# GpSimd takes the elementwise preparation of early chunks, and chunk 5's keys come as rows

## The chip, the cores and the metric

The kernel runs on one core of a Trainium2 chip. The core has five engines with a queue each, worked off in order: TensorE (PE in the profile: matrix products; PEld is its loading of weights), VectorE (DVE), ScalarE (ACT), GpSimd (POOL) and SyncE (SP, which issues DMAs here). The metric is the device time of one execution in microseconds. Three executions of the kernel before took 847.1, 846.52 and 846.56 us, median 846.56.

## The reference

Three parts, one feeding the next, all in float32. First a linear attention with decay over 4 batches, 8 heads, 768 steps and 48 channels:

```
for t in range(S):
    cur = einsum(u * k[t], v[t])
    y[t] = einsum(r[t], state + cur)
    state = w * state + einsum(k[t], v[t])
```

Its output, 3072 tokens of 384 numbers, goes through a maximum of three products (`max(x@w1, x@w2, x@w3) @ w_out`, 768 wide) and then through a mixture of 8 experts in which each token goes to the two best of its noisy gates.

## The kernel before, in words

**Chunks and blocks.** The tokens are cut into 24 chunks of 128 (six to a batch). Attention works by chunk. The middle part works by block of three chunks (8 blocks). Block b runs 21 units: 18 steps `u_step` (a product for each of six column groups f and three weights j; k = 3f + j) and three steps `x2_step`, units 18 to 20, that multiply by `w_out` and the gates. While block b runs, the attention of later chunks is put between its units by a table BURSTS: at unit (b, k) stand the output of one chunk and the scores of the next. For block 0 these are (0,2): output 3, scores 4; (0,9): output 4, scores 5; (0,17): output 5, scores 6.

**Preparing a chunk.** `prep1(g)` makes two tiles on VectorE: `Pk`, k times a table of decays (L389), and `Rp`, r times another (L390). `prep2(g)` makes what the state and the bonus (the term with u) need. For chunks below NPE = 6 it makes r times k (L401, tile `t1`), and then `keys(g)` lets TensorE turn and scale the keys with a diagonal matrix (L430, 16 products) and sum the bonus (L435, 16 products); ScalarE copies the result (L436) and scales v by it (L443). For later chunks the keys come from memory as rows in a tile `ldt` (L247) and VectorE does all: product of r and k (L406), the keys times a table (L408), times u (L409), the sum by head (L410), times v (L411, tile `sv`). The table is made in units 9 and 12 of block 0. The output of a chunk is taken out of PSUM with `sv` added (L498). The last chunk of a batch, as chunk 5, passes on no state.

**Weights.** In block 0 VectorE also decodes the 24 weight tiles (L1568 to L1570, three instructions each, generator `conv`) and subtracts the high parts that ScalarE makes (L672) to get the low parts (L673, generator `splits`). A counter `room` decides how many such instructions `fill` emits in a unit. Block 0's `u_step` multiplies in full float32 (L734); its results are taken out by ScalarE for j = 0 (L741) and by a maximum on VectorE for j = 1 and 2 (L745, tile `uw`); after j = 2 ScalarE makes `hHt` (L747) and VectorE `hLt` (L749), which the `x2_step` reads (L765 to L767; it needs the last group in its last three products). Later blocks use L736 to L738.

**Order.** Everything is in the order in which the program emits it (a manual schedule): each engine's queue holds its instructions in that order. In blocks 0 and 1 a generator `agen` of preparation instructions is advanced once a unit, or as often as STEPS says for that unit, and is emptied every seven units; loads of chunk g + 2 are issued at those units too, through SP's queue, in which a load waits until its buffer is free and holds up what is behind it. POOL makes constants at the start and issues the scatters of rows to the experts, six per block.

Of the kernel before, what the change touches and what calls it, by code (L numbers as in the profile page):

```python
# [34 lines left out]
CAPS = (816, 848, 816, 800, 784, 784, 768, 768)  # L35
ROW = DM + E + 1
NWST = 12
NPE = 6


BURSTS = {(0, 2): ([3], [4]), (0, 9): ([4], [5]), (0, 17): ([5], [6]), (1, 2): ([6], [7]), (1, 9): ([7], [8]),
# [3 lines left out]
PLAIN = (8,)  # L45
XTR = 19
TURN = 5
STEPS = {(0, 1): 2, (0, 2): 0, (1, 8): 2, (1, 10): 0}
SCATTER = 11
FLAGS = 5  # L50
TABK = 12
# [23 lines left out]
def gap(k):  # L75

    k = k.rearrange("p (a c) -> p a c", a=4)
    return bass.AP(tensor=k.tensor, offset=k.offset, ap=[k.ap[0], [DP, 4], [64, 2], [1, 48]])
# [125 lines left out]
def moe_kernel(ctx, tc, rT, kT, tm, wuT, wrow, urow, mw, wout, wgn, noise, ew1, ew2, out):  # L204
    nc = tc.nc
    v = nc.vector
# [22 lines left out]
    def cols():  # L229

        return at.tile([128, DM], F32, name="cols", bufs=6)

    def load_rk(g, eng=nc.sync):

        l = LD[g] = Ctx()
        l.r = at.tile([DP, 4, 128], F32, name="ldr", tag="ldr", bufs=3)
        (nc.sync if g < 2 else eng).dma_start(l.r, rT[:, g])
        l.k = at.tile([DP, 4, 128], F32, name="ldk", tag="ldk", bufs=3)
        eng.dma_start(l.k, kT[:, g])

    def load_tv(g, eng=nc.sync):

        l = LD[g]
        rows = tm[g * C:(g + 1) * C]
        if g >= NPE:
            l.t = at.tile([128, DM + 4 * DP], F32, name="ldt", tag="ldt", bufs=2)
            eng.dma_start(l.t, rows[:, :DM + 4 * DP])  # L247
        l.v = cols()
        eng.dma_start(l.v, rows[:, DM + 4 * DP:])

    def load(g, eng=nc.sync):
        load_rk(g, eng)
        load_tv(g, eng)
# [90 lines left out]
    Tr, Tk = T[:, :, 0:128], T[:, :, 127::-1]  # L344
# [35 lines left out]
    def hd(ap):  # L380
        return ap.rearrange("p (h d) -> p h d", h=H)

    def prep1(g):

        l = LD[g]
        a = A_[g] = Ctx()
        a.Pk = at.tile([DP, 4, 128], F32, name="Pk", bufs=2)
        a.Rp = at.tile([128, 4, 128], F32, name="Rp", tag=f"Rp{int(g > 9 and g // 2 % 2)}", bufs=2)[:DP]
        yield v.tensor_mul(a.Pk, l.k, Tk)  # L389
        yield v.tensor_mul(a.Rp, l.r, Tr)  # L390

    def prep2(g):

        l, a = LD[g], A_[g]
        a.v = l.v
        a.K2 = at.tile([128, 4 * DP + 8], F32, name="K2", bufs=2)
        a.sv = at.tile([128, DM], F32, name="sv", bufs=2)
        t1 = at.tile([128, 512], F32, name="t1", tag="t1")
        if g < NPE:
            a.t1 = t1[:DP].rearrange("p (a c) -> p a c", a=4)  # L400
            yield v.tensor_mul(a.t1, l.r, l.k)  # L401
            return
        t1 = t1[:, :DM]
        tr, tk = l.t[:, :DM], l.t[:, DM:DM + 4 * DP]
        red = at.tile([128, H, 1], F32, name="red")
        yield v.tensor_mul(t1.rearrange("p (a b d) -> p a b d", a=4, b=2),  # L406
                           tr.rearrange("p (a b d) -> p a b d", a=4, b=2), gap(tk))
        yield v.tensor_mul(a.K2[:, :4 * DP], tk, TAB["k"])  # L408
        yield v.tensor_mul(t1, t1, ub)  # L409
        yield v.tensor_reduce(red, hd(t1), axis=AX.X, op=OP.add)  # L410
        yield v.tensor_mul(hd(a.sv), hd(a.v), red.to_broadcast([128, H, D]))  # L411

    def prep(g):

        yield from prep1(g)
        yield from prep2(g)
        if g < NPE:
            keys(g)
            if g > 3:
                yield  # L420
            yield
            bonus(g)
# [15 lines left out]
    def bonus(g):  # L438

        a = A_[g]  # L440
        for h in range(H):
            hs = slice(h * D, h * D + D)
            nc.scalar.activation(a.sv[:, hs], a.v[:, hs], AF.Copy, scale=a.K2[:, 4 * DP + h:4 * DP + h + 1])  # L443
# [218 lines left out]
    split_done = [0]  # L662
# [13 lines left out]
    splits = split_all()  # L676

    def until(gen, done, n):
        while done[0] < n and next(gen, gen) is not gen:
            pass  # L680
# [580 lines left out]
    order = list(FEED)  # L1261
    agen, ahead = iter(()), None

    def splits_may(k):

        return 24 if k > 16 else min(len(WGT) + 2, 6) if WGT else 0
# [15 lines left out]
    for b in range(NBLK):  # L1282
        side = {}

        def add(k, fn):
            side.setdefault(k, []).append(fn)

        for k, i in XSK.get(b, {}).items():
            add(k, lambda i=i: init_xs(i))
        if b in (2, 3):  # L1290
            for i in range(OUTP // 2):
                add(4 * i + 1, lambda i=i + (b - 2) * (OUTP // 2): init_out(i))
        for g, q in TURNS.items():
            if q // 21 == b:
                add(q % 21, lambda g=g: x_turn(g))
        if b == NBLK - 1:
            ats.close()
            pools[0] = fast.enter_context(tc.tile_pool(name="ma", bufs=1, side="right"))
            e_alloc(0)
            for i in range(3):  # L1300
                add(2 * i, lambda i=i: e_load(0, i))
            for i in range(8):
                add(3 + 2 * i, lambda i=i: e_high(0, i))
                add(4 + 2 * i, lambda i=i: e_low(0, i))
                if i + 3 < 8:
                    add(4 + 2 * i, lambda i=i: e_load(0, i + 3))
            add(8, lambda: g_load(0, 0))
            add(17, lambda: g_gate(0, 0))
            for k in range(3):
                add(16 + k, lambda k=k: g_tr(0, 0, k))  # L1310
                add(17 + k, lambda k=k: g_low(0, 0, k))
        for k, (kind, f, j) in enumerate(units):
            ready = []
            unit[0] = k
            g = 3 * (b + 1) + k // 7
            if b < 2 and k % 7 == 0:
                load(g + 2)
                drain(agen)
                agen = ahead or prep(g + 1)
                ahead = None  # L1320
            here = BURSTS.get((b, k))
            if here:
                if b > 1:
                    drain(FEED[order.pop(0)].gen)
                if len(here[1]) > 1 or len(here[0]) > 1:
                    while reading[0]:
                        next(rgen)
                    settle()
                ready, late = burst(*here)
                defer.extend(late)  # L1330
            elif b < NBLK - 1 and k == XTR and not bounced(3 * b + 5):
                ready.append(xtr(3 * b + 5))
            if kind and j == 0:
                drain(rgen)
            evs = u_step(b, f, j) if kind == 0 else x2_step(b, j)
            settle()
            if defer and not here:
                defer.pop(0)()
            for fn in side.get(k, []):
                fn()  # L1340
            room = min(max(room, -1.0), 0.5) + ((1.46 if b else 2.3) - 0.47 if kind == 0 else 2.9 if b else 2.2)
            if 1 < b < NBLK - 1:
                room += (2.5 if len(here[0]) > 1 else 1.7) if here else spare(b, k) - ((1.46 - 0.47) if kind == 0 else 2.9)
            elif b < 2:
                room += (1.7 if len(here[0]) < 2 else 2.5) if here else 0.0
                room -= 0.4
            elif k % 2 == 0 and 3 < k < 20:
                room -= 0.9
            if b == 0 and k == 17:

                room = min(room, 0.5)
            if here:
                fill(b, k)
            for fn in ready:
                fn()
            waiting += evs
            if b < 2:
                take(agen, STEPS.get((b, k), 1))
                if k >= XTR and b == 0:
                    ahead = ahead or prep(g + 2)  # L1360
                    next(ahead, None)
            if b and order:
                room -= FEED[order[0]].step(b, k)
            if b == 0:
                until(conv, conv_done, min(k + 2, 18) if k < 13 else min(2 * k - 6, 24))
                if k in (TABK - 3, TABK):
                    tables2()
                for f in GATEM.get(k, ()):
                    wg_mm(f)
                for f in GATEK.get(k, ()):  # L1370
                    wg_tr(f)
                if k == 16:
                    until(splits, split_done, 6)
                    wg_out()
                if k == 17:
                    settle()
                if k == 20:
                    until(splits, split_done, 7)
            if b == 1:
                until(splits, split_done, min(k + 8, 24))  # L1380
            fill(b, k)
        settle()
        settle()
        rgen = route(b)
# [374 lines left out]
```

## Time and profile before

| | |
|---|---|
| median of three runs | 846.56 us |
| the profiled execution | 845.93 us, its span (first to last instruction) 844.1 us |
| TensorE busy | 828.3 us, 98% of the span |
| VectorE busy | 527.3 us, 62% |
| ScalarE busy | 283.7 us, 34% |
| GpSimd busy | 137.5 us, 16% |
| mean granted TensorE clock | 0.997 |

Shares are means over the whole program. Block 0 runs from about 24 to 90 us, block 1 from there to about 140 us. A row of the timeline gives the start, the time from the first start to the last end of the merged instructions, the engine, the line, the operation, what it writes and reads, and in brackets the idle time of that engine just before, with what ended it. VectorE's instructions overlap a little at their ends, so the distance between two starts is the time that one takes of the queue.

### The profile page before, as it was taken

The numbers are of one execution on the slowest core, as the hardware profiler recorded it, in microseconds if no ns is written. First come the engines' busy times: TensorE is split into PE (matmuls) and PEld (weight loads), VectorE is DVE, ScalarE is ACT, GpSimd is POOL, SyncE is SP. The second block draws the span as 40 slices with busy tenths as digits, with TensorE's granted clock in tenths as the row PEclk, the third lists the DMA queues.
The fourth block names the chain that finished last, engine by engine and source line by source line (L and its number), as shares of the span: only waits on it lengthen the run. The fifth ranks groups of instructions, "written<-read, shape, count | busy, mean of one in ns | idle before, by whom it ended". The sixth has DMA issues, their size and how long they took to land.

```text
span 844.1 us, 17138 instructions
## 1 busy us (share of the span) xinstructions
PE 828.3 (98%) x6657; PEld 772.7 (92%) x6657; DVE 527.3 (62%) x1394; ACT 283.7 (34%) x600; POOL 137.5 (16%) x124
## 2 busy tenths in 40 slices
PE   8999999999999999999999999999999999999995
PEld 6667999999999999999999999999999999999994
DVE  8997987878777786647637662654626446254320
ACT  6334432123221222124215542434424344243221
POOL 1000030020202011111223130220312203122121
PEclk9999999999999999999999999999999999999998
DMA  8991262574433322135129783662655626463222
GB/s 248 350 276 38 84 208 92 180 242 154 162 111 126 103 89 77 40 112 142 48 83 220 193 191 85 144 152 83 126 124 134 156 79 135 112 150 40 51 30 31
DMA packets 102558, 109.79 MB, mean 130 GB/s; under 512 B 58322, under 2 KB 85315, under 8 KB 102467
## 3 DMA queue, kind: packets, MB, share of 16 engines
q1 hardware_dynamic: 91602, 88.65, 37.0%
q0 software_dynamic: 10320, 19.10, 10.9%
q8 instruction: 54, 0.88, 0.4%
q10 hardware_dynamic: 544, 0.85, 0.4%
q14 instruction: 38, 0.30, 0.1%
HBM read 74.95 MB, written 33.99 MB: 129 GB/s over the span
## 4 chain that ended last, share of the span: by engine, by line
PE 88%; issue 4%; DVE 4%; DMA 1%; POOL 1%; ACT 0%; SPq 0%; POOLq 0%; DVEq 0%
PE b_u L736 8%; PE b_u L737 7%; PE b_u L738 7%; PE b_u L982 7%; PE b_u L983 7%; PE b_u L984 7%; PE b_u L734 3%; PE b_sc L455 2%; PE b_y L477 2%; PE b_y L1010 1%; PE b_y L1011 1%; PE b_st L1012 1%; PE b_x L1010 1%; PE b_tx L1012 1%; PE b_st L1010 1%
## 5 line engine op out<-in xcount | busy, mean ns | idle before, releaser
L994 DVE SCALAR_TENSOR_TENSOR ghL<-b_u,ghH 128x512 fp32r<-128x512 f32 (+5 forms) x120 | 70.0, 583 | 189.3 <-ACT ghH L993 189.3
L982 PE MATMUL b_u<-gxH,e1H 128*128 128x512 f32 (+5 forms) x384 | 132.8, 346 | 0.0
L983 PE MATMUL b_u<-gxL,e1H 128*128 128x512 f32 (+5 forms) x384 | 131.9, 344 | 0.0
L984 PE MATMUL b_u<-gxH,e1L 128*128 128x512 f32 (+5 forms) x384 | 131.8, 343 | 0.0
L736 PE MATMUL b_u<-xHt,wH 128*128 128x384 f32 x378 | 128.7, 340 | 0.6 <-DVE uw L745 0.6
L737 PE MATMUL b_u<-xLt,wH 128*128 128x384 f32 x378 | 127.0, 336 | 0.0
L738 PE MATMUL b_u<-xHt,wl 128*128 128x384 f32 x378 | 126.8, 335 | 0.0
L993 ACT ACTIVATE ghH<-b_u 128x512 fp32r<-128x512 f32 (+5 forms) x120 | 61.4, 511 | 157.9 <-PE b_u L984 151.9
L827 POOL DMA_INDIRECT XS<-rows,ii x48 | 50.1, 1043 | 383.0 <-issue 191.3
L984 PEld LDWEIGHTS b_u<-gxH,e1L 128*128 128x128 f32 x384 | 72.2, 188 | 8.9
L982 PEld LDWEIGHTS b_u<-gxH,e1H 128*128 128x128 f32 x384 | 72.3, 188 | 6.2
L983 PEld LDWEIGHTS b_u<-gxL,e1H 128*128 128x128 f32 x384 | 72.2, 188 | 5.9
L736 PEld LDWEIGHTS b_u<-xHt,wH 128*128 128x128 f32 x378 | 70.9, 188 | 2.9 <-issue 1.2
L1075 POOL DMA_INDIRECT out_dram<-ys,gix x34 | 53.2, 1564 | 125.5 <-ACT ys L1106 118.2
L745 DVE TENSOR_TENSOR uw<-b_u,uw 128x384 f32<-128x384 f32 x96 | 53.3, 555 | 28.9 <-PE b_u L738 26.0
L737 PEld LDWEIGHTS b_u<-xLt,wH 128*128 128x128 f32 x378 | 71.0, 188 | 0.0
L738 PEld LDWEIGHTS b_u<-xHt,wl 128*128 128x128 f32 x378 | 70.9, 188 | 0.0
L747 ACT ACTIVATE hHt<-uw 128x384 fp32r<-128x384 f32 x48 | 25.2, 525 | 129.6 <-DVE uw L745 126.3
L1075 POOL DMA_INDIRECT out_dram<-yrows,gix x20 | 30.6, 1528 | 189.6 <-ACT yrows L1069 185.6
L949 ACT ACTIVATE gxH<-raw 128x512 fp32r<-128x512 f32 (+4 forms) x48 | 26.0, 543 | 77.7 <-DVE raw L948 75.5
L741 ACT ACTIVATE uw<-b_u 128x384 f32<-128x384 f32 x48 | 23.5, 489 | 31.5 <-PE b_u L738 26.7
L734 PE MATMUL b_u<-xHt,wl 128*128 128x384 f32 x96 | 32.8, 492 | 1.0 <-DVE uw L745 1.0
(309 smaller groups left out, 1778.1 us busy)
## 6 DMA issues: line engine op xcount, KB each, us to landing
est<-in_ew_dram SPq DMA_DIRECT2D x64, 384.0 KB, 4.4
ldt<-in_tm_dram SPq DMA_DIRECT2D x18, 416.0 KB, 3.5
raw<-XS SPq DMA_DIRECT2D x32, 192.0 KB, 4.3
ldr<-in_rT_dram SPq DMA_DIRECT2D x24, 224.0 KB, 5.1
wS<-in_w_dram SPq DMA_DIRECT2D x14, 384.0 KB, 6.0
ldk<-in_kT_dram SPq DMA_DIRECT2D x22, 224.0 KB, 4.9
out_dram<-zrow SPq DMA_DIRECT2D x8, 576.0 KB, 4.7
cols<-in_tm_dram SPq DMA_DIRECT2D x22, 192.0 KB, 4.1
```

The source lines that it names most:

```text
L734: nc.tensor.matmul(o, WF[3 * f + j][:, ks], xH[b][:, k, :], start=(k == 0), stop=(k == 2))
L736: nc.tensor.matmul(o, WH[j][:, f, ks], xH[b][:, k, :], start=(k == 0), stop=False)
L737: nc.tensor.matmul(o, WH[j][:, f, ks], xL[b][:, k, :], start=False, stop=False)
L738: nc.tensor.matmul(o, WL[3 * f + j][:, ks], xH[b][:, k, :], start=False, stop=(k == 2))
L745: v.tensor_tensor(w, o, w, op=OP.max)
L827: st = nc.gpsimd.indirect_dma_start(out=XS, out_offset=bass.IndirectOffsetOnAxis(ap=ii[:, 3 * k + j:3 * k + j + 1], axis=0), in_=rw[:, j, ...
L982: nc.tensor.matmul(u, a[:, k, fs], o.xH[:, k, :n], start=(k == 0), stop=False)
L983: nc.tensor.matmul(u, a[:, k, fs], o.xL[:, k, :n], start=False, stop=False)
L984: nc.tensor.matmul(u, b[:, k, fs], o.xH[:, k, :n], start=False, stop=(k == 2))
L993: nc.scalar.activation(hH[:, :n], u, AF.Relu)
L994: v.scalar_tensor_tensor(hL[:, :n], u, 0.0, f32(hH[:, :n]), op0=OP.max, op1=OP.subtract)
L1075: st = nc.gpsimd.indirect_dma_start(out=out, out_offset=bass.IndirectOffsetOnAxis(ap=o.ix[:o.n[j], j, :], axis=0), in_=ys, in_offset=None, ...
```

## The change

NPE becomes 5, so that chunk 5 takes the way of rows. `Pk` and `Rp` of chunks 4, 5 and 6 and `t1` of chunks 0 to 4 are made by GpSimd. In block 0 the preparation is ordered anew: from unit 14 on come chunk 6's scalings, then all five row instructions of chunk 5 in unit 16, then chunk 6's. Chunk 7's row tile and values are loaded at unit 17 instead of 14. In unit (0,2) the decoding ahead of the evacuations is left to the end of the unit. In block 1 chunk 8's preparation takes three steps in unit 8 and none in unit 9, and one more split may be emitted at unit 8.

```diff
-NPE = 6
+NPE = 5
+AHEAD = 7
-STEPS = {(0, 1): 2, (0, 2): 0, (1, 8): 2, (1, 10): 0}
+STEPS = {(0, 0): 2, (0, 2): 0, (0, 14): 2, (0, 15): 0, (0, 16): 5, (1, 8): 3, (1, 9): 0}
...
-        yield v.tensor_mul(a.Pk, l.k, Tk)
-        yield v.tensor_mul(a.Rp, l.r, Tr)
+        e = nc.gpsimd if 3 < g < AHEAD else v
+        yield e.tensor_mul(a.Pk, l.k, Tk)
+        yield e.tensor_mul(a.Rp, l.r, Tr)
...
-            yield v.tensor_mul(a.t1, l.r, l.k)
+            yield nc.gpsimd.tensor_mul(a.t1, l.r, l.k)
...
+    def between56():
+
+        yield from prep1(6)
+        yield from prep2(5)
+        yield from prep2(6)
...
+            if (b, k) == (0, 17):
+                load_tv(7)
             if b < 2 and k % 7 == 0:
-                load(g + 2)
+                (load_rk if (b, k) == (0, 14) else load)(g + 2)
                 drain(agen)
-                agen = ahead or prep(g + 1)
+                agen = ahead or (between56() if 21 * b + k == 14 else prep1(5) if 21 * b + k == 7 else prep(g + 1))
...
-            if here:
+            if here and (b, k) != (0, 2):
                 fill(b, k)
...
-                until(splits, split_done, min(k + 8, 24))
+                until(splits, split_done, min(k + 8 + (k == 8), 24))
```

## Rows read from the trace of the kernel before

**Rows 1.** The page's busy times: us, share of the span, instructions

```profile
PE 828.3 (98%) x6657; PEld 772.7 (92%) x6657; DVE 527.3 (62%) x1394; ACT 283.7 (34%) x600; POOL 137.5 (16%) x124
```

**Rows 2.** Waits of PE: who waited for whom, us, times, longest

```profile
PE b_x L430 <- issue: 1.0, 1, 1.0
...
PE b_u L734 <- DVE uw L745: 1.0, 1, 1.0
PE b_u L736 <- DVE uw L745: 0.6, 1, 0.6
```

**Rows 3.** Busy us by engine in a stretch, instructions, clock, DMA share, GB/s

```profile
30.00:40.00 10.00, 8.86 (x106) 6.10 (x102) 9.96 (x24) 1.59 (x5) 0.00 (x0) 1.00 1.04 336
```

**Rows 4.** Chain that ended last, 55 to 58 us: start, us, what

```profile
55.99 0.92 PE b_x L430 x16
56.91 0.41 PE b_x L435 x15
```

**Rows 5.** Timeline of VectorE, 26 to 38 us

```profile
26.64 1.29 DVE L464 TENSOR_TENSOR A<-b_sc,maskS 128x512 f32<-128x512 f32 x2
27.85 0.68 DVE L389 TENSOR_TENSOR Pk<-ldk,T 112x512 f32<-112x512 f32 x1
...
30.12 0.69 DVE L390 TENSOR_TENSOR Rp<-ldr,T 112x512 f32<-112x512 f32 x1
30.73 0.69 DVE L401 TENSOR_TENSOR t<-ldr,ldk 112x512 f32<-112x512 f32 x1
...
37.83 0.55 DVE L745 TENSOR_TENSOR uw<-b_u,uw 128x384 f32<-128x384 f32 x1
```

**Rows 6.** Timeline of TensorE, 30 to 39 us

```profile
30.95 1.10 PE L455 MATMUL b_sc<-Rp,Pk 48*64 48x128 f32 x32 [0.17 <-DVE Rp L390]
...
38.43 9.94 PE L734 MATMUL b_u<-xHt,wl 128*128 128x384 f32 x30 [0.97 <-DVE uw L745]
```

**Rows 7.** Timeline of VectorE, 72 to 83 us

```profile
72.56 1.50 DVE L673 TENSOR_TENSOR wol<-wol,woH 128x384 fp32r<-128x384 f32 x3 [3.63 <-ACT woH L672]
...
74.44 0.55 DVE L406 TENSOR_TENSOR t<-ldt 128x384 f32<-128x384 f32 x1
...
80.34 0.62 DVE L408 TENSOR_TENSOR K<-ldt,tabs 128x448 f32<-128x448 f32 x1
80.87 0.55 DVE L745 TENSOR_TENSOR uw<-b_u,uw 128x384 f32<-128x384 f32 x1
...
82.02 0.56 DVE L749 TENSOR_TENSOR hLt<-uw,hHt 128x384 fp32r<-128x384 f32 x1
82.49 0.55 DVE L409 TENSOR_TENSOR t<-t,ub 128x384 f32<-128x384 f32 x1
```

**Rows 8.** Timeline of TensorE, at 82 us

```profile
82.63 0.45 PE L767 MATMUL b_x<-woH,hLt 128*128 128x400 f32 x1
```

**Rows 9.** Timeline of GpSimd, 2 to 113 us

```profile
2.29 0.80 POOL L352 MEMSET St<- 112x384 f32 x2
3.04 0.14 POOL L354 IOTA eidx<- 128x8 f32 x1
...
112.44 1.16 POOL L827 DMA_INDIRECT XS<-rows,ii  x1 [109.00 <-DVE x L495]
```

**Rows 10.** Timeline, the first chunk's scaling and scores

```profile
6.12 0.69 DVE L390 TENSOR_TENSOR Rp<-ldr,T 112x512 f32<-112x512 f32 x1
...
6.86 1.10 PE L455 MATMUL b_sc<-Rp,Pk 48*64 48x128 f32 x32 [0.24 <-DVE Rp L390]
```

**Rows 11.** Timeline of VectorE and TensorE, 109 to 116 us

```profile
109.77 0.56 DVE L673 TENSOR_TENSOR wl<-wl,wH 128x384 fp32r<-128x384 f32 x1 [1.00 <-ACT wH L672]
113.83 0.62 DVE L408 TENSOR_TENSOR K<-ldt,tabs 128x448 f32<-128x448 f32 x1
115.30 0.55 DVE L745 TENSOR_TENSOR uw<-b_u,uw 128x384 f32<-128x384 f32 x1
...
115.90 0.45 PE L736 MATMUL b_u<-xHt,wH 128*128 128x384 f32 x1 [0.59 <-DVE uw L745]
```

## The prediction

> **What bounds the kernel now.** Read the shares of the page first: TensorE (PE) is busy 98% of the span, 828.3 us [rows 1]. So a change can give time back in two ways only: less work on PE, or a gap of PE closed. Then the waits of PE: outside the start they are few, 1.0 us in a matmul group where the profile names no releaser, 1.0 us of the first block's u products (L734) and 0.6 us of the second block's (L736), both on VectorE's (DVE) maximum `uw` [rows 2]. Then the table by stretch: from 30 to 40 us DVE is busy 9.96 of 10 us, PE 8.86, GpSimd (POOL) nothing [rows 3]. So in the stretch that the change touches PE sets the end nearly everywhere, DVE holds it up in two places, and POOL is empty.
>
> **The change part by part.**
> *Chunk 5 off TensorE.* Its keys leave PE: 16 products with the diagonal and 16 of the bonus, which on the chain of waits take 0.92 + 0.41 = 1.33 us [rows 4]. They stand on the chain itself, so I count all of it: -1.33. ScalarE loses one copy and eight scaled copies; no wait of PE in [rows 2] is on ScalarE, so nothing.
>
> *DVE relieved before 38 us.* DVE loses r times k of chunks 3 and 4 and both scalings of chunk 4. One such instruction starts 0.61 us before the next (30.12 to 30.73) [rows 5]; four are 2.4 us, all before the `uw` at 37.83 for which PE sat idle 0.97 us [rows 5, 6]. If POOL does not slow DVE, that `uw` comes early enough and the gap goes: -0.97. The 0.17 us in which the scores of chunk 4 wait for DVE's `Rp` [rows 6] goes too, if POOL has `Rp` by 30.8: -0.17. The moved fill at unit (0,2) only puts six decoding instructions behind the evacuations instead of ahead of them; all of them still stand before that `uw`, so 0. After this PE is next limited by itself.
>
> *POOL's price.* The trace of before has no elementwise instruction on POOL. Nearest rows: two memsets of 112x384 start 0.75 us before the next instruction, 0.375 each, so about 1 ns an element [rows 9]. One pass over 512 elements is then 0.5 us; three passes one after the other (two reads, one write) are 1.6. I take 1.1, the middle; an instruction with two inputs can hardly be at the low end. Eleven of them are 12 us of an engine that is idle from 4 to 112 us [rows 9]. Loads of chunk 4 are on the chip by 27.85, where DVE starts on them without a wait [rows 5]; even from there two POOL instructions of 1.1 end at 30.05 and leave 0.7 us (at 1.6 they would end at 31.05, 0.3 late). Chunks 5 and 6 are made 10 us or more ahead of their scores, so a wait there is worth 0. Queued on POOL behind them is nothing until the scatters at 112 us [rows 9].
>
> *The rows of chunk 5 on DVE.* Five new instructions (product with r, scaling by the table, product with u, sum, product with v), all issued in unit (0,16) because the evacuation of chunk 5's output in unit (0,17) needs the last. The scaling is 0.53 (80.34 to 80.87) and the others, of 128x384, are 0.47 each (82.02 to 82.49): 2.41 us [rows 7]. DVE does have a hole of 3.63 us just before, but it ends when ScalarE delivers `woH`, and three splits wait in the queue for that, ahead of the new five [rows 7]. So the five land behind the hole, in a stretch in which DVE does not idle from 72.56 to the `hLt` at 82.02 [rows 7]. PE's product of unit 18 waits for that `hLt`: it starts at 82.63 just as `hLt` ends, without slack [rows 8]. What else moves in that stretch: the product of chunk 6 goes one unit later, still ahead of `hLt`, and chunk 6's scaling (0.53) moves behind it. Net 2.41 - 0.53 = +1.88 on PE. Below it is bounded by 0, if the hole takes the five after all, and above by 2.41.
>
> *Loads.* Chunk 5 gets a row tile of 416 KB and chunk 7's waits in SP's queue for chunk 5's scaling instead of following at once. What is queued behind is two clearings of `XS` (needed at the first scatter, 112 us) and chunk 8's loads (first used in unit (1,7)): covered, 0. Without that cover chunk 7's product in unit (1,0) would be late.
>
> *Second block's order.* Chunk 8's scaling moves from behind the evacuation in (1,9) to ahead of it, and its product with u from behind the `uw` of unit 10 to ahead of it. PE waited 0.59 us for that `uw` [rows 11]. Counted in the queue, the scaling cancels (0.53 out, 0.53 in, both ahead of that `uw`) and the product adds 0.47; against it stands DVE's idle 1.00 us at 109.77 [rows 11], which a different phase might fill. Bounds +0.47 and -0.59; I take 0. The extra split allowed at unit 8 changes nothing: counted in the order of emission, 20 of 24 splits are issued before it.
>
> *Sum.* -1.33 - 0.97 - 0.17 + 1.88 = -0.59 us. The profiled execution took 845.93 us (span 844.1), 0.63 under the median of 846.56 that I predict against; the difference is carried over: 846.56 - 0.59 = 846.0.
>
> **The rivals.**
> *A: the row work hides (faster).* If DVE reaches unit 16 with its lead, and the splits and the five fit before PE needs `hLt`, the 1.88 falls away: 846.56 - 2.47 = 844.1, and 843.5 with the gap of [rows 11] closed as well. For it: DVE is freed of nine instructions, 5.5 us, before 68 us and has the 3.63 us hole. Against it: the hole's end follows PE and ScalarE, not DVE, and the queue is in order.
>
> *B: POOL holds DVE up (slower).* While a POOL instruction that reads two inputs runs, DVE instructions with two SBUF inputs stand still. Place one: POOL's first product can start when r of chunk 0 lands, while DVE makes `Rp` at 6.12, and PE starts on that `Rp` at 6.86 with DVE as releaser [rows 10]: +1.1 straight on PE. Place two: the three instructions of chunk 4, 3.3 us, fall on the decoding at 27 to 31 us; the masking at 26.64 reads PSUM and covers some 0.4; minus the 2.4 saved that is +0.5, and the gap of 0.97 stays. Sum 1.1 + 0.5 - 1.33 + 1.88 = +2.15: 848.7. With POOL at 0.5 us it would be +0.1, at 1.6 us +4. It decides from the point where one POOL instruction costs DVE more than the 0.6 us that it saves. The trace cannot say, since no POOL instruction reads SBUF there before 112 us. The Trainium skill ("SBUF — State Buffer", section "Who interferes with whom") speaks for it: it says that a VectorE instruction with two SBUF inputs contends with a GpSimd instruction that reads SBUF, and that the second to issue blocks until the first is done; no run shown yet bears on it. The skill's price ("GPSIMD Engine Reference", section "Elementwise — side-by-side cycle accounting") is 4497 ns for 2048 elements, an estimate of 1.12 us for 512, by which rival B would come to the same 848.7. Against B: nothing in the rows, only that 2.4 to 5.5 us of DVE time are given back on the way.
>
> **How the numbers follow.** Less than 0.2% (1.7 us) cannot be told from no change here: faster means below 844.9, slower above 848.2. The forecast (846.0, no change) gets 0.43, rival A 0.31, rival B 0.26; B at a cheap POOL ends in "no change", and half costs of the 1.88 lie between forecast and A. Chances: faster 0.33, same 0.43, slower 0.24. The range goes from 843.6 (A with the second gap nearly closed) to 848.9 (B at 1.1 us a piece); the forecast's own is 844.9 to 847.0.
>
> **What would show it.** Right: no L430 and L435 of a sixth chunk and 1.33 us less of them; PE's wait on `uw` at unit 4 gone; a new PE wait of some 1.9 us near 80 us on DVE's `hLt` or ScalarE's `hHt` (L765 or L767); the hole of DVE before the first `woH` split longer than 3.6 us. Rival A: no such wait. Rival B: DVE rows with two SBUF inputs longer than 0.55 to 0.69 us beside POOL rows, and the first scores later than 6.86 us. I am wrong in kind if PE waits on POOL itself, or if DVE loses its hole before 72 us.

## The result, and the profile after

The changed kernel takes 850.44 us (median of 12; 848.94 to 857.67) against 846.45 us of before beside it (12 runs, 845.6 to 848.88): ratio 1.0063, 95% interval 1.0043 to 1.0082. It is slower, by 4.0 us. Its twelve executions fall in two groups, seven at 848.94 to 851.34 and five at 854.27 to 857.67. The profiled one took 849.54 us (span 847.8), so it belongs to the first.

The page's busy times, to be read against [rows 1]:

```profile
PE 829.0 (98%) x6625; PEld 771.4 (91%) x6625; DVE 527.9 (62%) x1387; ACT 281.5 (33%) x591; POOL 156.4 (18%) x135
```

TensorE has 32 products fewer and is as busy as before, GpSimd has its eleven instructions and 19 us more. What has grown is TensorE's waits, which answer to [rows 2]; the columns are who waited for whom, us in all, times, longest:

```profile
PE b_x L767 <- ACT hHt L749: 1.5, 1, 1.5
PE b_x L432 <- ACT xHt L629: 1.4, 1, 1.4
PE b_u L738 <- DVE uw L747: 1.4, 2, 1.1
PE b_u L736 <- DVE uw L747: 1.2, 2, 0.7
```

Lines have moved by two or so (L455 is now L457, L734 is L736, L745 is L747). The places of these waits, and what runs beside them, from the timeline of the changed kernel, 5 to 119 us:

```profile
5.21 1.27 POOL L403 TENSOR_TENSOR t<-ldr,ldk 112x512 f32<-112x512 f32 x1 [1.76 <-DMA ldr<-in_rT_dram]
5.29 1.73 DVE L391 TENSOR_TENSOR Pk<-ldk,T 112x512 f32<-112x512 f32 x1
6.95 0.68 DVE L392 TENSOR_TENSOR Rp<-ldr,T 112x512 f32<-112x512 f32 x1
7.68 1.10 PE L457 MATMUL b_sc<-Rp,Pk 48*64 48x128 f32 x32 [0.40 <-DVE Rp L392]
...
16.83 0.99 PE L432 MATMUL b_x<-tabs,Pk 112*64 112x112 f32 x16 [1.44 <-ACT xHt L629]
...
28.27 1.18 POOL L392 TENSOR_TENSOR Rp<-ldr,T 112x512 f32<-112x512 f32 x1
28.50 1.36 DVE L1579 SCALAR_TENSOR_TENSOR wl<-wS,wl 128x384 int32<-128x384 int32 x1
29.40 1.59 POOL L403 TENSOR_TENSOR t<-ldr,ldk 112x512 f32<-112x512 f32 x1
29.78 2.09 DVE L1580 SCALAR_TENSOR_TENSOR wl<-wS,wl 128x384 int32<-128x384 int32 x2
...
39.17 6.07 PE L736 MATMUL b_u<-xHt,wl 128*128 128x384 f32 x18 [0.71 <-DVE uw L747]
39.82 3.22 POOL L391 TENSOR_TENSOR Pk<-ldk,T 112x512 f32<-112x512 f32 x1 [8.83 <-DMA ldk<-in_kT_dram]
42.38 2.53 DVE L1580 SCALAR_TENSOR_TENSOR wl<-wst,wl 128x384 int32<-128x384 int32 x2
43.01 1.50 POOL L392 TENSOR_TENSOR Rp<-ldr,T 112x512 f32<-112x512 f32 x1
45.71 0.59 PE L736 MATMUL b_u<-xHt,wl 128*128 128x384 f32 x1 [0.46 <-DVE uw L747]
...
72.51 1.50 DVE L675 TENSOR_TENSOR wol<-wol,woH 128x384 fp32r<-128x384 f32 x3 [4.72 <-ACT woH L674]
...
76.56 0.56 DVE L413 TENSOR_TENSOR sv<-cols,red 128x384 f32<-128x384 f32 x1
...
84.07 0.56 DVE L751 TENSOR_TENSOR hLt<-uw,hHt 128x384 fp32r<-128x384 f32 x1
84.09 0.45 PE L767 MATMUL b_x<-woH,hHt 128*128 128x400 f32 x1 [1.48 <-ACT hHt L749]
84.55 0.62 DVE L410 TENSOR_TENSOR K<-ldt,tabs 128x448 f32<-128x448 f32 x1
...
93.46 0.54 DVE L413 TENSOR_TENSOR sv<-cols,red 128x384 f32<-128x384 f32 x1
...
101.45 0.44 PE L738 MATMUL b_u<-xHt,wH 128*128 128x384 f32 x1 [0.37 <-DVE uw L747]
...
118.93 0.45 PE L738 MATMUL b_u<-xHt,wH 128*128 128x384 f32 x1 [1.06 <-DVE uw L747]
```

Read the top rows first. GpSimd's first product starts 0.08 us ahead of VectorE's `Pk`, and `Pk` takes 1.73 us instead of 0.69: it ends 0.54 us after GpSimd's product. `Rp` comes at 6.95 instead of 6.12 and the first scores at 7.68 instead of 6.86 [rows 10]. At 28 to 31 us the decoding beside GpSimd is stretched in the same way: 1.36 us for one instruction that takes 0.55 elsewhere, 2.09 for two that take 1.02 in the kernel before:

```profile
28.92 1.02 DVE L1570 SCALAR_TENSOR_TENSOR wl<-wS,wl 128x384 int32<-128x384 int32 x2
```

The gap before unit 4 is still there, 0.71 us for 0.97 [rows 6]. GpSimd is held up too (3.22 us at 39.82). Nobody waits for that product, but the ones of chunk 5 hold up VectorE once more: beside them two decoding instructions take 2.53 us (42.38), the next maximum is late, and TensorE waits 0.46 us at 45.71, where the kernel before has no wait.

Where the same TensorE instruction starts, in us, and how far the profiled kernels on chips as fast as this one are behind (+) or ahead (-) there. The last four columns are runs of the next section; "decoding later" is the second one under "A better order":

| start in before | | after | r k of chunk 0 back | no product on GpSimd | only products on GpSimd | decoding later |
|---|---|---|---|---|---|---|
| 6.86 | scores of chunk 0 | +0.82 | +0.16 | +0.20 | +1.00 | +0.35 |
| 30.95 | scores of chunk 4 | +1.01 | -0.25 | -0.02 | +4.61 | +0.23 |
| 50.82 | scores of chunk 5 | +1.47 | +0.19 | +0.21 | +4.88 | -0.82 |
| 61.22 | tables, after chunk 5's keys | -0.05 | -1.34 | -1.02 | +4.99 | -0.81 |
| 76.38 | scores of chunk 6 | -0.06 | -1.34 | -1.03 | +5.09 | -0.82 |
| 94.54 | scores of chunk 7 | +2.07 | +0.78 | +1.11 | +5.09 | -0.81 |
| 109.30 | scores of chunk 8 | +2.55 | +1.27 | +1.62 | +5.09 | -0.81 |
| 126.15 | scores of chunk 9 | +3.02 | +1.73 | +2.08 | +5.08 | -1.03 |

The column "after" is the whole story of the first 130 us: 1.47 lost where 1.14 should have been won (half of it, 0.73, between unit 4 and 49 us, at the wait at 45.71), 1.52 won with the keys, 2.1 lost at 84 us, 0.97 lost in block 1. From there to 413 us it stays at 3.0; the experts' part adds 0.4 to 0.8.

### The profile page after: what moved, and what is told of

The parts are those of the page before. It is cut to its first block, busy times and chain, and to the rows that moved or that the text cites. A ratio compares the mean times of both kernels' runs of the same rounds, so it can differ in the third digit from the quotient of the medians.

```text
span 847.8 us, 17085 instructions
## 1 busy us (share of the span) xinstructions
PE 829.0 (98%) x6625; PEld 771.4 (91%) x6625; DVE 527.9 (62%) x1387; ACT 281.5 (33%) x591; POOL 156.4 (18%) x135
## 4 chain that ended last, share of the span: by engine, by line
PE 83%; DVE 7%; issue 5%; DMA 1%; POOL 1%; ACT 1%; SPq 0%; POOLq 0%; DVEq 0%; ACTq 0%
PE b_u L738 7%; PE b_u L985 7%; PE b_u L984 7%; PE b_u L986 7%; PE b_u L739 7%; PE b_u L740 7%; PE b_u L736 2%; PE b_y L479 1%; PE b_sc L457 1%; PE b_y L1012 1%; PE b_y L1013 1%; PE b_st L1014 1%; PE b_x L1012 1%; PE b_tx L1014 1%; PE b_st L1012 1%
## 5 line engine op out<-in xcount | busy, mean ns | idle before, releaser
L747 DVE TENSOR_TENSOR uw<-b_u,uw 128x384 f32<-128x384 f32 x96 | 53.2, 554 | 27.9 <-PE b_u L740 25.0
L736 PE MATMUL b_u<-xHt,wl 128*128 128x384 f32 x96 | 32.8, 492 | 1.2 <-DVE uw L747 1.2
```

Source lines behind the costliest of these rows:

```text
L736: nc.tensor.matmul(o, WF[3 * f + j][:, ks], xH[b][:, k, :], start=(k == 0), stop=(k == 2))
L747: v.tensor_tensor(w, o, w, op=OP.max)
```

## The experiments

Theory: a GpSimd product of two SBUF tiles holds up VectorE's instruction beside it, and that takes back what the moved work gives; the rows of chunk 5 cost what was predicted. Rival: GpSimd is harmless and order or waits explain all.

**One product back.** The changed kernel, r times k of chunk 0 on VectorE again.

```diff
-            yield nc.gpsimd.tensor_mul(a.t1, l.r, l.k)
+            yield (nc.gpsimd if g else v).tensor_mul(a.t1, l.r, l.k)
```

> The changed kernel with r times k of chunk 0 alone back on VectorE. If a GpSimd instruction that reads SBUF holds up VectorE's instructions with two SBUF inputs (theory H), the first scaling takes 0.6 us again instead of 1.66, the first scores start at 6.6 to 6.9 us instead of 7.68, and the time falls by 0.8 us, with up to 0.4 more if the wait before the third chunk's keys (16.83 us) shrinks too. If the loss comes only from the order of VectorE's queue (theory Q), the first scores stay near 7.7 us and nothing changes. Of the five of twelve executions near 856 us: if they come from the late start they go, else some remain.

849.3 us (six executions, 848.31 to 852.23; before 846.18), ratio 1.0038 (1.0023 to 1.0052). The late start goes:

```profile
7.02 1.10 PE L457 MATMUL b_sc<-Rp,Pk 48*64 48x128 f32 x32
```

No idle time stands in front, and until 456 us the kernel is 1.3 us ahead of the changed one. Of that, 0.66 is at the first scores, and 0.6 more at the stop ahead of the keys of chunk 2:

```profile
15.56 0.99 PE L432 MATMUL b_x<-tabs,Pk 112*64 112x112 f32 x16 [0.83 <-issue]
```

It is 0.83 us long here, 1.44 in the changed kernel (16.83 above). What that stop waits for stays open, so no more than the 0.66 is shown to be the price of the one product. The wait beside chunk 5's products is there again (0.45 us at 44.42, behind decoding of 2.53 us). Little of the 1.3 us reaches the end: in the experts' part TensorE idles again (0.10 us in 460 to 465, 0.40 in 465 to 470, where the changed kernel has none) and the lag is 3.2 us from 500 us on. The cause of that stays open.

**No product on GpSimd.** The changed kernel with all eleven products back on VectorE; order and rows of chunk 5 as changed.

```diff
-        e = nc.gpsimd if 3 < g < AHEAD else v
+        e = v
...
-            yield nc.gpsimd.tensor_mul(a.t1, l.r, l.k)
+            yield v.tensor_mul(a.t1, l.r, l.k)
```

> The changed kernel with all eleven GpSimd products back on VectorE: chunk 5's rows and the new order alone. Theory H: no VectorE instruction before 62 us above 0.7 us, first scores at 6.86 us; TensorE's work falls by the 1.5 us of chunk 5's keys, the gap before unit 4 is back at about 1 us, the wait of 1.5 to 2 us for the last hidden group stays, and so do the 0.96 us of block 1: 846.5 - 1.5 + 2.1 + 0.9 = 848.0. Theory Q: the whole loss is still there, 849.5.

848.73 us (five, 848.29 to 850.77), ratio 1.0037 (1.0024 to 1.0049). TensorE's waits:

```profile
PE b_x L767 <- ACT hHt L749: 1.5, 1, 1.5
PE b_u L738 <- DVE uw L747: 1.4, 2, 1.1
PE b_u L736 <- DVE uw L747: 1.2, 1, 1.2
```

The stall at 84 us and both waits of block 1 are there without GpSimd: they belong to the rows and the order, and with them about 2.5 of the 4.0 us. The gap before unit 4 is 1.2 us; the second wait on L736 is gone, and the two decoding instructions at that place take 1.02 us again. At 61 us this kernel is 1.02 us ahead of before, the changed one 0.05: with GpSimd's products 0.97 us is lost there instead of any won (0.41 of it lies in the stop ahead of chunk 2's keys, 1.44 us for 1.03).

**Only the products on GpSimd.** The kernel before; Pk and Rp of chunks 4 to 6 and r times k of chunks 0 to 5 on GpSimd: twelve products, one more than in the changed kernel.

```diff
+        e = nc.gpsimd if 3 < g < 7 else v
+        yield e.tensor_mul(a.Pk, l.k, Tk)
+        yield e.tensor_mul(a.Rp, l.r, Tr)
...
+            yield nc.gpsimd.tensor_mul(a.t1, l.r, l.k)
```

> The kernel before with the eleven products moved to GpSimd and nothing else: chunk 5's keys stay on TensorE, order and steps as before. Theory H: first scores 0.8 us late, VectorE rows of 1.3 to 1.7 us beside GpSimd's, the gap before unit 4 not closed, together +1.0 to +1.5 us against the kernel before, and no new wait at 84 us nor in block 1: 847.5 to 848.0. Theory Q: VectorE is 6.6 us lighter, the gap before unit 4 closes: 845.5.

850.16 us (six, 849.12 to 853.05), ratio 1.0047 (1.0031 to 1.0063): 4.0 us, where 1.0 to 1.5 was expected. The three executions with a mean granted clock of 0.995 to 0.997 take 849.1 to 849.3 us, the three at 0.992 and 0.993, the profiled one (851.01) among them, 851.0 to 853.1. Its timeline, 27 to 32 us:

```profile
27.86 1.24 POOL L390 TENSOR_TENSOR Pk<-ldk,T 112x512 f32<-112x512 f32 x1 [7.93 <-DMA ldk<-in_kT_dram]
27.97 2.60 DVE L1569 TENSOR_SCALAR wl<-wS 128x384 int32<-128x384 int32 x2
29.05 1.30 POOL L391 TENSOR_TENSOR Rp<-ldr,T 112x512 f32<-112x512 f32 x1
30.31 1.38 POOL L402 TENSOR_TENSOR t<-ldr,ldk 112x512 f32<-112x512 f32 x1
30.49 1.62 DVE L1570 SCALAR_TENSOR_TENSOR wl<-wS,wl 128x384 int32<-128x384 int32 x1
```

Three VectorE instructions take 4.2 us beside three of GpSimd; they take 1.2 (0.62 for two, 0.55) elsewhere. The first two read one tile only and are held up as well. The next mask comes too late, TensorE waits 1.22 us for it (at 32.89). From 14 us to the scores of chunk 4 this execution falls from 1.1 to 4.6 us behind: 0.4 in the stop ahead of chunk 2's keys, 1.6 from there to the scores of chunk 3, and 1.5 beside the products shown. The 1.6 is TensorE's clock: it had stood still for 1.44 us ahead of the keys of chunk 2, and 18 to 21 us has a granted clock of 0.55 (mostly the lower level, 1.2 of 2.4 GHz), where before has 1.00. The columns are the stretch, the sum, the five engines' busy time, clock, DMA share and GB/s:

```profile
18.00:21.00 3.00, 3.00 (x61) 3.00 (x60) 0.34 (x1) 2.45 (x10) 1.28 (x1) 0.55 0.03 8
```

**Reading by itself, and writing by itself.** The kernel before, all its work where it was, plus idle GpSimd work at the same places. The first adds products of two 112x384 tiles into a scratch tile:

```diff
+            if g < 5:
+                nc.gpsimd.tensor_mul(scr, l.r[:, :3], l.k[:, :3])
```

> The kernel before, in which VectorE does everything as before, plus idle work on GpSimd: a product of two 112x384 tiles into a scratch tile that nobody reads, one where r times k of chunks 0 to 4 is made and two where Pk and Rp of chunks 4 to 6 are. Nothing is taken from VectorE and nobody waits for GpSimd. Theory (a GpSimd product of two SBUF tiles holds VectorE up): VectorE's Pk or Rp of chunk 0 lasts 1.3 to 1.7 us instead of 0.69, the first scores start at 7.4 to 7.9 instead of 6.86, VectorE's decoding near 28 to 31 us is stretched and the gap before unit 4 (0.97) grows by 1 us or more; the whole 1 to 4 us over the kernel before. Rival (what slows the changed kernel is the order, or the wait for GpSimd's results): no VectorE row stretched, first scores at 6.86, time within 0.5 us of before.

The second adds a product of one element a partition, which waits for the same loads, and then memsets of the scratch tile:

```diff
+            if g < 5:
+                nc.gpsimd.tensor_mul(scr[:, 0, 0:1], l.r[:, 0, 0:1], l.k[:, 0, 0:1])
+                nc.gpsimd.memset(scr, 0.0)
+                nc.gpsimd.memset(scr, 0.0)
```

> The same as the run with idle products on GpSimd, but at each of those places GpSimd does a product of one element a partition (which waits for the same loads) and then two or four memsets of the scratch tile, so that it is busy at the same times but reads next to nothing. Theory (it is GpSimd's reading beside VectorE that costs): no VectorE row beside the memsets longer than 0.7 us, first scores at 6.9 to 7.1, time within 0.7 us of before. Rival (any GpSimd work at these times slows VectorE, or its instructions cost the others something else): rows stretched as with the idle products, first scores at 7.4 or later, 1 to 4 us over before.

These two, the run with more idle products on TensorE and the first of the better orders ran on a chip on which before takes 860.57 us (23 executions), with a granted clock of 0.99 in the mean; they are compared with that and with one another. Idle products: 865.01 us, ratio 1.0059 (1.004 to 1.0078). Idle memsets: 860.61 us, ratio 1.0001 (0.9987 to 1.0015). The start with idle products:

```profile
4.96 1.24 POOL L406 TENSOR_TENSOR scr<-ldr,ldk 112x384 bf16<-112x384 f32 x1 [1.51 <-DMA ldr<-in_rT_dram]
5.26 0.96 DVE L346 TENSOR_TENSOR w<-T 112x4 f32<-112x4 f32 x1
6.14 0.68 DVE L393 TENSOR_TENSOR Pk<-ldk,T 112x512 f32<-112x512 f32 x1
6.82 1.46 POOL L406 TENSOR_TENSOR scr<-ldr,ldk 112x384 bf16<-112x384 f32 x1 [0.62 <-DMA ldr<-in_rT_dram]
7.35 1.48 DVE L407 TENSOR_TENSOR t<-ldr,ldk 112x512 f32<-112x512 f32 x1
```

and with idle memsets:

```profile
5.25 0.69 DVE L396 TENSOR_TENSOR Pk<-ldk,T 112x512 f32<-112x512 f32 x1
5.32 0.42 POOL L410 MEMSET scr<- 112x384 bf16 x1
5.80 0.42 POOL L411 MEMSET scr<- 112x384 bf16 x1
5.86 0.68 DVE L397 TENSOR_TENSOR Rp<-ldr,T 112x512 f32<-112x512 f32 x1
```

In the first, even an instruction on 4 columns (0.16 us in before) lasts until GpSimd's product is over, and not `Pk` but that one was hit, since here the product came 0.25 us earlier. In the second, from 4 to 62 us, VectorE's products and decoding are at their usual length but for one `TENSOR_SCALAR` (0.66 us for 0.35, at 40.67 beside a memset). The scores of chunk 4 start at 33.72 and 31.66 us, those of chunk 9 at 129.10 and 126.82: 2.3 us for work that nobody waits for. So it is shown what holds VectorE's products up: GpSimd's reading, apart from order and from waits for GpSimd. By the rule cited in the prediction ("SBUF — State Buffer" of the Trainium skill, "Who interferes with whom") only a GpSimd instruction that reads is in the way of a VectorE instruction with two SBUF inputs, not one that only writes, and the second to issue waits; these two traces agree, with 0.96 against 0.16 us and with 0.69 us unchanged.

**The order of block 1.** The changed kernel with chunk 8's product with u behind the maximum of unit 10 again, and chunk 6's leftover earlier.

```diff
-STEPS = {(0, 0): 2, (0, 2): 0, (0, 14): 2, (0, 15): 0, (0, 16): 5, (1, 8): 3, (1, 9): 0}
+STEPS = {(0, 0): 2, (0, 2): 0, (0, 14): 2, (0, 15): 0, (0, 16): 5, (0, 20): 2, (1, 8): 2, (1, 10): 0}
```

> The changed kernel with chunk 6's last row instruction back in unit (0,20) and chunk 8's steps in block 1 as before. Both theories: the wait of 0.37 us at 101.4 us goes and the one at 118.9 us falls from 1.06 to 0.6 us; 0.9 us less than the changed kernel, 848.5 for its faster executions. If the order of block 1 costs nothing, as the prediction took it, the time does not move.

849.12 us (848.24 to 849.18 four times, 851.2, 855.98), ratio 1.0036 (1.0023 to 1.0049). TensorE's two waits in block 1 are 1.1 us together, the longer 0.6, for 1.4 and 1.06:

```profile
PE b_u L738 <- DVE uw L747: 1.1, 2, 0.6
```

So the product with u ahead of that maximum cost its 0.47 us. The other wait (0.49, for 0.37) stays, although chunk 6's last product here ends before block 1 starts: VectorE has the same work in a stretch without idle time, and where in it that product stands makes no difference. The profile happens to be of the execution of 855.98 us, the only long one that was profiled:

```profile
7.99 1.98 PE L457 MATMUL b_sc<-Rp,Pk 48*64 48x128 f32 x32 [0.71 <-DVE Rp L392]
9.91 1.76 PE L432 MATMUL b_x<-tabs,Pk 112*64 112x112 f32 x16
```

32 score products take 1.98 us for 1.10, the keys 1.76 for 0.99, and so on until 19 us, from where all is as usual; by then it is 6.0 us behind. The granted clock is shown as 1.00 in the whole stretch.

**What sets off the long executions.** Three more idle products ahead of the changed kernel's first scores, so that TensorE does not idle there:

```diff
-WARM0 = 11
+WARM0 = 14
```

> The changed kernel with 14 instead of 11 idle products on TensorE at the start, so that these end at or after the first Rp and TensorE does not idle ahead of the first scores. Theory (the executions of 854 to 858 us come from TensorE idling between these products and the late first scores, after which it works at half rate for some 11 us): all executions between 848.5 and 851.5 us, first scores at 7.7 to 8.4 us, none above 853. Rival (those executions have another cause): a third or more of them still lie at 854 to 858 us.

863.1 to 865.05 us three times, 871.58 to 873.09 three times (before there 860.57). The theory falls: the long ones come just as often without the idle time. Two idle products fewer in the kernel before (WARM0 = 9):

> The kernel before with 9 instead of 11 idle products on TensorE at the start, so that it idles 0.6 to 1.2 us ahead of the first scores and nothing else differs. Theory (the executions of the changed kernel that take some 5 us longer come from such an idle stretch, after which TensorE works at half rate for 11 us): a third or more of the executions lie 4 to 8 us above the others, and a profile of one of those has the first scores at 1.98 us for 32 products instead of 1.10. Rival (they come from the later waits, ahead of the keys of chunk 2, or from GpSimd at work): all executions within 1.5 us of the kernel before beside it.

848.49 us (twelve; four at 845.35 to 846.58, eight at 848.38 to 849.36; before 846.16), ratio 1.0017 (1.0005 to 1.0029). Neither theory nor rival: no stretch at half rate from the first scores on, but a lower clock after a later stop.

```profile
14.96 0.41 PE L430 MATMUL b_x<-tabs,Pk 112*64 112x112 f32 x2
16.87 0.83 PE L430 MATMUL b_x<-tabs,Pk 112*64 112x112 f32 x13 [1.51 <-issue]
```

```profile
18.00:21.00 3.00, 3.00 (x53) 3.00 (x53) 0.07 (x1) 2.55 (x10) 0.00 (x0) 0.50 0.02 7
```

TensorE stands still for 1.51 us, and at 18 to 21 us the granted clock is 0.50 (1.2 GHz); from 22 us it is 1.00, and the kernel 2.8 us behind. Last, the kernel before with nothing but r times k of chunk 0 on GpSimd:

```diff
-            yield v.tensor_mul(a.t1, l.r, l.k)
+            yield (v if g else nc.gpsimd).tensor_mul(a.t1, l.r, l.k)
```

> The kernel before with one instruction moved: r times k of chunk 0 is made by GpSimd, everything else as before. Theory (a single GpSimd product at 5.3 us, beside VectorE's Pk of chunk 0, is enough for the late start, and the late start for executions about 5 us longer): Pk lasts 1.6 to 1.8 us instead of 0.69, the first scores start at 7.5 to 8.0 us instead of 6.86, at 48 us the program is 0.4 to 1.1 us behind before, and of a dozen executions some lie 4 to 8 us above the others. Rival (the longer executions need the other GpSimd products too, or the longer pause ahead of the keys of chunk 2 that they bring): the same late start, all executions within 1.5 us of one another, median 0.3 to 1.2 us over before.

863.45 us (twelve, 860.98 to 865.94) on a chip with before at 861.78 (17), ratio 1.0012 (0.9994 to 1.0031): by the time, unclear. Its executions spread over 5 us without two groups. The timeline is clear:

```profile
5.30 1.40 POOL L401 TENSOR_TENSOR t<-ldr,ldk 112x512 f32<-112x512 f32 x1 [1.85 <-DMA ldr<-in_rT_dram]
5.50 1.23 DVE L346 TENSOR_TENSOR w<-T 112x4 f32<-112x4 f32 x1
7.99 1.10 PE L455 MATMUL b_sc<-Rp,Pk 48*64 48x128 f32 x32 [1.67 <-DVE Rp L390]
```

One product, and the first scores are late by 1.1 us against before, by 0.8 against the run with idle memsets, which starts them at 7.21. What sets off the executions that are some 5 to 9 us longer stays open: they were seen in kernels with the products of chunks 0 to 4 on GpSimd (5 of 12, 1 of 6, 3 of 6), and in none of the eleven executions of the first two experiments or the six with only the products moved.

**A better order.** The kernel before, no GpSimd product, chunk 5 as before, and VectorE's two late maxima attacked by order alone. First, two decoding instructions go ahead of chunk 1's output, and chunk 8's scaling behind the maximum of unit 10:

```diff
+    take(conv, 2)
     y1()
...
-    take(conv, 2)
...
-STEPS = {(0, 1): 2, (0, 2): 0, (1, 8): 2, (1, 10): 0}
+STEPS = {(0, 1): 2, (0, 2): 0, (1, 8): 2, (1, 9): 0, (1, 10): 0}
```

> The kernel before with order alone changed, nothing on GpSimd and chunk 5 as before: the two decoding instructions behind the preparation of chunk 3 are emitted ahead of chunk 1's output, where VectorE idled 1.21 us, and in block 1 chunk 8's scaling is made two units later, behind the maximum of unit 10. Theory (the gaps of 0.97 us before unit 4 and of 0.59 us in block 1 are VectorE being late by that much): the first shrinks to 0.4 or less, the second to 0.1, the time 0.8 to 1.3 us under before, 845.2 to 845.6. Rival (the gaps come back later, at the next point where VectorE is late): no change by the end of the program, within 0.4 us of before, with other waits of TensorE on VectorE of the same size.

860.84 us, before 860.57, ratio 0.9998 (0.9984 to 1.0013): no change that can be told. The trace shows a gain: from 48 us on it is 0.65 us ahead of the idle memsets, 0.83 us at the scores of chunk 9. But 0.78 us of the gap before unit 4 is left; that of block 1 is gone. Second, the same STEPS, and three decoding instructions of unit (0,2) left for later units:

```diff
             if here:
+                if (b, k) == (0, 2):
+                    room -= 1.41
                 fill(b, k)
```

> The kernel before with order alone changed, nothing on GpSimd and chunk 5 as before: in unit (0,2) three decoding instructions fewer are emitted ahead of the evacuations (they come units later; 3 x 0.47 us), and chunk 8's scaling in block 1 is made behind the maximum of unit 10. Theory (the gap of 0.97 us before unit 4 and that of 0.59 us in block 1 are only VectorE's order; that the earlier order run moved the first gap by 0.2 us only is because its decoding went ahead of a wait for TensorE): the first gap goes to 0.1 or less and does not come back before 80 us, the second to 0.1 or less; 1.2 to 1.6 us under before. Rival (VectorE is short of time as such in block 0): the gap comes back at a later maximum or at the end of the decoding, within 0.5 us of before.

**844.55 us** (eleven, 843.66 to 845.14; before 846.16 of 29), ratio 0.9978 (0.9969 to 0.9987): the fastest of all. TensorE's waits are the start's only:

```profile
PE b_tx L330 <- POOL wz L324: 2.4, 1, 2.4
PE b_x L430 <- issue: 0.8, 1, 0.8
PE b_sc L455 <- DVE Rp L390: 0.2, 1, 0.2
```

Unit 4 starts at 37.61 without a gap [rows 6], unit 11 of block 1 too [rows 11], and neither comes back. Last, on top of it, ScalarE's scaled copies of chunk 1 behind the keys of chunk 2:

```diff
+        if g == 2:
+            bonus(1)
         nc.scalar.activation(a.K2, pk[:, :4 * DP + 8], AF.Copy)
```

> The run with three decoding instructions fewer in unit (0,2), plus: ScalarE's eight scaled copies of chunk 1's v are emitted behind TensorE's products of chunk 2's keys instead of ahead of them (no work added or taken). Theory (TensorE's 1.0 us ahead of the keys of chunk 2, for which the trace of before names no releaser, is a wait for those copies: they end at 15.6 us, the keys start at 15.57): the keys of chunk 2 start at 14.6 and 0.5 to 1.0 us more are saved, 1.7 to 2.6 us under before. Rival (the wait is for something else): the keys still start at 15.5 or later, time as of the run without this.

845.21 us, ratio 0.9988 (0.9979 to 0.9997). The rival holds: the keys still wait 1.01 us (16.08), so it was not those copies, and the time is no better than without the move.

## Why the prediction was wrong

846.0 us was forecast, 850.4 came; the range ended at 848.9.

- **The keys of chunk 5**: -1.33 predicted, -1.52 measured (from +1.47 at the scores of chunk 5 to -0.05 at the tables; -1.23 in the kernel without GpSimd products). Right.
- **The five rows**: +1.88 predicted, +2.11 measured at 84 us, with the wait named (L767 on `hHt`); `hLt` starts at 84.07 as PE restarts, and both stand behind the maximum `uw`, which comes at 82.93 for 80.87. The hole before `woH` did grow to 4.72 us and hid nothing. Right, and independent of GpSimd.
- **VectorE relieved before 38 us** is the step that failed: "If POOL does not slow DVE". It was taken as the condition of the forecast, and it does not hold. Instead of -0.97 and -0.17 the kernel is 1.47 us late at 51 us: 0.82 at the first scores, 0.44 more at the keys of chunk 2 (the stop whose cause is open), 0.52 won back up to unit 4, and 0.73 lost at 45.71, beside chunk 5's products. This is the mechanism of rival B, but not its sizes. At place one it said +1.1; after shows +0.82, the kernel with that product alone 0.8 to 1.1, and kernels without it start the scores anywhere from 6.86 to 7.21. At place two it said +0.5 with the whole gap left; 0.52 was won, and 0.71 us of the gap is left. Chunk 5's products, whose price the prediction set at 0 because nobody waits for them, are in neither sum. That rival B's 1.6 us for GpSimd comes near the 1.47 is in part luck.
- **POOL's price**, 1.1 us: measured 1.18 to 1.30 where nothing was in its way. The Trainium skill's price ("GPSIMD Engine Reference", "Elementwise — side-by-side cycle accounting") gave an estimate of 1.12; both are a little low.
- **Block 1**, taken as 0 between +0.47 and -0.59: measured +0.97, outside the bounds. The 0.47 for the product with u came in full (second wait 1.06 for 0.59). The other half is a wait of 0.37 us at 101.45 that before does not have, and it goes back to the term "2.41 - 0.53": chunk 6's scaling, moved behind `hLt` (84.55; 80.34 in [rows 7]), was taken as gone. It pushes chunk 6's later steps on by one, the last (`sv`, 93.46) into block 1, and VectorE has no idle time between 88 us and the late maximum to take it up. The run with the other order shows that its place there does not matter.
- **Not foreseen**: the executions at 854 to 858 us, and that the lag grows again among the experts.

By the sum, rival B's 848.7 plus the 0.97 of block 1 is 849.7; the first group of executions has its middle at 849.5. The sum fits better than its terms do. The mechanism was in the text and had 0.26; with the rule at hand and no row against it, it should have been the forecast.

## What to carry to other kernels

Work moved to an idle engine is free only if that engine does not stand in another's way: price it by what it holds up, at the moment it runs, and look first at the chain that starts the kernel. An idle copy of the moved work, read by nobody, measures that price in one run. Where VectorE is late by less than a microsecond for one instruction, look first for work ahead of it in its queue that is not due: three decoding instructions put off, with one scaling of block 1 moved behind a maximum, won 1.6 us here; eleven moved to GpSimd won nothing.

## What the runs showed of the hardware that was not expected

- A GpSimd product held up VectorE's `TENSOR_SCALAR`, which reads one tile (2.60 us for two, 0.62 elsewhere), and one on 112x4 (0.96 and 1.23 us, 0.16 elsewhere) as well as one on 112x512 (1.73 us, 0.69 elsewhere).
- It works the other way round too: GpSimd's products of one element a partition, beside VectorE's work, took 0.28 to 3.08 us.
- TensorE stops at about 15 us, 0.8 to 1.7 us long, in every profile but that of the long execution. One stop comes after two of sixteen like products (14.96, 16.87 above), so it is probably not for data, and the releaser named there is then chance; this is not shown. It is 0.83 to 1.17 us long in seven of the eight profiles without a GpSimd product ahead of the first scores (1.51 with two idle products fewer), 1.23 to 1.70 in the five with one. Where the stop was 1.44, 1.51 and 1.70 us long, in the run with only the products, in that with two idle products fewer and in that with one product moved, the granted clock was 0.50 to 0.61 behind it; after one of 1.01 us (before) it stayed at 1.00, and after one of 1.44 us in the changed kernel too.
- TensorE ran at little over half its rate for 11 us (32 products in 1.98 us for 1.10) with a granted clock shown as 1.00.
